# Attention of four heads at a time in 64x64 array tiles, two heads per partition half

## Chip, cores and metric

One core of one Trainium2 chip. The metric is the device time of the program in microseconds (us); lower is better. Every comparison is with runs of the kernel before on the same chip.

In the lines of the profile PE is TensorE, PEld its weight loads, DVE VectorE, ACT ScalarE, POOL GpSimd, whose queue issues the loads, and SP the queue of the output stores and the DMA transposes. The first two numbers are start and duration in us; a bracket such as [3.51 <-DMA x_sb<-xT] is the engine's idle time just before and what ended it. To evict is to copy a result out of PSUM, the memory that TensorE writes; to land is to arrive, for a transfer; a slot is the time that the array needs for one matmul. A burst is the group of loads that one step sends.

## The reference

Attention without softmax, then a mixer block, for 8 batches, 12 heads, 448 tokens and a head size of 64:

```python
scores = scale * np.matmul(q, k.transpose(0, 1, 3, 2))
attn = np.maximum(scores, 0.0) ** 2 / S
x = np.matmul(attn, v)                     # heads side by side: (8, 448, 768)
h = np.maximum(x.transpose(0, 2, 1) @ w_tok1, 0.0) @ w_tok2   # token mix, 448 -> 256 -> 448
u = x + h.transpose(0, 2, 1)
out = u + np.maximum(u @ w_ch1, 0.0) @ w_ch2                  # channel mix, 768 -> 1536 -> 768
```

## The kernel before

It works on a pair of heads per step, 48 steps. `x` comes out of the attention with channels on partitions (`xT`); token 1 needs it with tokens on partitions, so `x_back` turns it, for later steps by a DMA transpose on the SP queue. Channel work (the largest part, 218 us of TensorE) is queued per batch and dealt out in portions by `fill` to keep TensorE busy. Program order is kept on every engine. The parts that matter, cut:

```python
    raw   = ...tile_pool(name="raw", bufs=6)
    ps_att = ...(bufs=2, PSUM)   # scores, two banks each
    ps_acc = ...(bufs=1, PSUM)   # values, one bank
    ps_mm  = ...(bufs=3, PSUM)   # everything else, one bank each

    def scores(s, blocks):       # 128 keys at a time, 64x128 tiles: one head per row half
        for c in blocks:
            for e in range(2):
                h = slice(64 * e, 64 * (e + 1))
                nc.tensor.matmul(ps[:, e, :S], lhsT=sb[h, KO + c*128 : KO + (c+1)*128],
                                 rhs=sb[h, :S], start=True, stop=True)
    # scores_rest: the last 64 keys of both heads in one 128x128 matmul, through the padded kz
    # values: 128x64 tiles; values_rest: one 128x128 matmul through the padded vz

    def x_back(s):
        if s >= XDMA:            # XDMA = 12
            nc.sync.dma_start_transpose(out=x_tiles[s // PG][:, p % PG], in_=xT[b % 2][:, p, :])
            return
        # ... earlier ones by TensorE

    for s in range(NS + 4):      # (cut)
        scores(s, (0, 1)); load_pair(s + PRE); transposes(s + 1); values(s - 1)
        scores(s, (2,)); values_rest(s - 1)
        if s - 1 >= XDMA: x_back(s - 1)
        square(); fill(0.25); scores_rest(s); fill(0.25); square()
        if (s - 3) % PG == PG - 1:
            token2(...)          # of the pairs s-4 and s-3
            if (s - 3) % NP == NP - 1: channel_work(...)     # queues it, and issues six u transposes
        fill(0.25)
        if (s - 2) % PG == PG - 1: token1((s - 2) // PG)     # pairs s-3 and s-2: x sent a step or two ago
        fill(0.25)
```

Of the kernel before, what the change touches and what calls it, by code (L numbers as in the profile page):

```python
# [16 lines left out]
def kernel(  # L17
# [11 lines left out]
    nc = tc.nc  # L29
# [7 lines left out]
    QC = 4  # L37
    QP = S // QC
    KB = 3
    KM = KB * 128  # L40
    KR = S - KM
# [11 lines left out]
    raw = ctx.enter_context(tc.tile_pool(name="raw", bufs=6))  # L53
# [5 lines left out]
    ps_mm = ctx.enter_context(tc.tile_pool(name="ps_mm", bufs=3, space=bass.MemoryType.PSUM))  # L59
# [4 lines left out]
    kz = [consts.tile([128, NP, 128], BF16, name=f"kz{i}") for i in range(2)]  # L64
    vz = [consts.tile([128, NP, 128], BF16, name=f"vz{i}") for i in range(2)]
# [7 lines left out]

    raws = {}

    def load_pair(s):
        b, p = divmod(s, NP)
        h0 = 2 * p
        q_raw = raw.tile([QP, 2, QC, D], BF16, name="q_raw")
        k_raw = raw.tile([128, 2, KB, D], BF16, name="k_raw")  # L80
        v_raw = raw.tile([128, 2, KB, D], BF16, name="v_raw")
        nc.gpsimd.dma_start(  # L82
            out=q_raw.rearrange("p h c d -> p h (c d)"),
            in_=q[b, h0 : h0 + 2].rearrange("h (p c) d -> p h (c d)", c=QC),
        )
        nc.gpsimd.dma_start(  # L86
            out=k_raw.rearrange("p h c d -> p h (c d)"),
            in_=k[b, h0 : h0 + 2, :KM].rearrange("h (p c) d -> p h (c d)", c=KB),
        )
        if s == 0:  # L90
            make_identity(nc, ident)
        if p == 0:
            load_rest(b, kz[b % 2], k)
        nc.gpsimd.dma_start(  # L94
            out=v_raw.rearrange("p h c d -> p h (c d)"),
            in_=v[b, h0 : h0 + 2, :KM].rearrange("h (p c) d -> p h (c d)", c=KB),
        )
        if p == 0:
            load_rest(b, vz[b % 2], v)
        raws[s] = (q_raw, k_raw, v_raw)  # L100

    def load_rest(b, dst, src):
        for e in range(2):
            nc.gpsimd.dma_start(
                out=dst[64 * e : 64 * e + KR, :, D * e : D * (e + 1)],
                in_=src[b].rearrange("(p e) s d -> e s p d", e=2)[e, KM:],
            )

    def load_wt1():
        w = moe_w_tok1.rearrange("(p c) j -> c p j", c=QC)  # L110
        for c in range(QC):
            lo = c * QP
            while lo < (c + 1) * QP:
                hi = min((c + 1) * QP, (lo // 128 + 1) * 128)
                r = lo % 128
                nc.gpsimd.dma_start(
                    out=wt1[r : r + hi - lo, lo // 128, :],
                    in_=w[c, lo - c * QP : hi - c * QP, :],
                )
                lo = hi  # L120
# [13 lines left out]
    def load_wc1(i):  # L134
        n = DC // 2
        nc.gpsimd.dma_start(
            out=wc1[:, :, i * n : (i + 1) * n],
            in_=moe_w_ch1.rearrange("(g p) n -> p g n", p=128)[:, :, i * n : (i + 1) * n],
        )

    def load_wc2(i):
        n = EC // 4
        nc.gpsimd.dma_start(
            out=wc2[:, i * n : (i + 1) * n, :],
            in_=moe_w_ch2.rearrange("(e p) n -> p e n", p=128)[:, i * n : (i + 1) * n, :],
        )


    qkT, at2, squares = {}, {}, []
    KO = S  # L150

    def transposes(s):
        b, p = divmod(s, NP)
        q_raw, k_raw, _ = raws[s]
        ps = ps_mm.tile([128, 1024], BF16, tag="bank", name="qkT_ps")
        blocks = [(c * QP, QP, q_raw[:, :, c, :]) for c in range(QC)]
        blocks += [(KO + c * 128, 128, k_raw[:, :, c, :]) for c in range(KB)]
        blocks.append(
            (KO + KM, 128, kz[b % 2][:, p, :].rearrange("n (h d) -> n h d", h=2))
        )  # L160
        for at, n, src in blocks:
            for h in range(2):
                nc.tensor.matmul(  # L163
                    ps[64 * h : 64 * (h + 1), at : at + n],
                    lhsT=src[:, h, :],
                    rhs=ident[:n, :n],
                    is_transpose=True,
                    start=True,
                    stop=True,
                    skip_group_check=True,  # L170
                )
        sb = attn.tile([128, KO + KM + 128], BF16, name="qkT")
        nc.vector.tensor_copy(sb, ps[:, : KO + KM + 128])  # L173
        qkT[s] = sb

    def relu2(s, key, ps, n):
        at = attn.tile([128, n, S], BF16, tag=f"at{n}", name="at", bufs=3)
        sq = attn.tile([128, n, S], BF16, tag=f"sq{n}", name="sq", bufs=3 * (3 if n == 2 else 1))
        nc.scalar.activation(at, ps[:, :, :S], AF.Relu)  # L179
        squares.append((at, sq))  # L180
        at2[s, key] = sq

    def square():
        for at, sq in squares:
            nc.vector.tensor_tensor(out=sq, in0=at, in1=at, op=ALU.mult)  # L185
        squares.clear()

    def scores(s, blocks):
        sb = qkT[s]
        made = []  # L190
        for c in blocks:
            ps = ps_att.tile([128, 2, 512], FP32, tag="att", name="sc_ps")
            for e in range(2):
                h = slice(64 * e, 64 * (e + 1))
                nc.tensor.matmul(  # L195
                    ps[:, e, :S],
                    lhsT=sb[h, KO + c * 128 : KO + (c + 1) * 128],
                    rhs=sb[h, :S],
                    start=True,
                    stop=True,  # L200
                )
            made.append((c, ps))
        for c, ps in made:
            relu2(s, c, ps, 2)

    def scores_rest(s):
        sb = qkT.pop(s)
        ps = ps_att.tile([128, 1, 512], FP32, tag="att", name="sr_ps")
        nc.tensor.matmul(  # L209
            ps[:, 0, :S],  # L210
            lhsT=sb[:, KO + KM : KO + KM + 128],
            rhs=sb[:, :S],
            start=True,
            stop=True,
        )
        relu2(s, KB, ps, 1)

    accs = {}

    def values(s):  # L220
        v_raw = raws[s][2]
        ps = ps_acc.tile([128, 512], FP32, name="acc_ps")
        for c in range(KB):
            sq = at2.pop((s, c))
            for e in range(2):
                nc.tensor.matmul(  # L226
                    ps[64 * e : 64 * (e + 1), :S],
                    lhsT=v_raw[:, e, c, :],
                    rhs=sq[:, e, :],
                    start=(c == 0),  # L230
                    stop=False,
                    skip_group_check=True,
                )
        accs[s] = ps

    def values_rest(s):
        b, p = divmod(s, NP)
        raws.pop(s)
        ps = accs.pop(s)
        nc.tensor.matmul(  # L240
            ps[:, :S],
            lhsT=vz[b % 2][:, p, :],
            rhs=at2.pop((s, KB))[:, 0, :],
            start=False,
            stop=True,
            skip_group_check=True,
        )
        nc.vector.tensor_scalar(  # L248
            out=xT[b % 2][:, p, :S],
            in0=ps[:, :S],  # L250
            scalar1=float(alpha2),
            scalar2=None,
            op0=ALU.mult,
        )
# [3 lines left out]
    PG = 2  # L258
    XDMA = 12

    def x_back(s):
        b, p = divmod(s, NP)
        if p % PG == 0:
            x_tiles[s // PG] = mix.tile([128, PG, 4, 128], BF16, name="x_sb")
        if s >= XDMA:
            nc.sync.dma_start_transpose(
                out=x_tiles[s // PG][:, p % PG], in_=xT[b % 2][:, p, :]
            )
            return
        ps = ps_mm.tile([128, 1024], BF16, tag="bank", name="x_ps")  # L270
        for c in range(4):
            nc.tensor.matmul(
                ps[:, c * 128 : (c + 1) * 128],
                lhsT=xT[b % 2][:, p, c * 128 : (c + 1) * 128],
                rhs=ident,
                is_transpose=True,
                start=(c == 0),
                stop=(c == 3),
            )
        nc.vector.tensor_copy(  # L280
            x_tiles[s // PG][:, p % PG],
            ps[:, :512].rearrange("n (c d) -> n c d", c=4),
        )

    def token1(i):
        x_sb = x_tiles.pop(i)
        ps = ps_mm.tile([128, JC, PG * 128], FP32, tag="bank", name="t1_ps")
# [9 lines left out]
        r1 = mix.tile([128, JC, PG * 128], BF16, name="r1_sb")  # L297
# [3 lines left out]
    def token2(s):  # L301
        b, p = divmod(s, NP)
# [204 lines left out]
```

## Time and profile before

| | kernel before |
|---|---|
| time, median | 413.6 us (413.0 to 415.0) |
| span of the profiled run | 411.6 us |
| TensorE busy | 388.3 us, 94% |
| first channel matmul at | 58.2 us |
| TensorE clock over the span | 0.98 |

The lines and their reading are in the prediction. Transposes by DMA, whose landing is in the view of the tile `x_sb`:

```profile
L266 SPq DMA_TRANSPOSE x_sb<-xT x36: 1189/1191/2271, 92.2 to 362.6; - x36
DMA to landing us min/median/max: 2.4/4.1/5.6
```

The first line gives the issue on the SP queue in ns (minimum, median, maximum), the second the time from issue to landing.

### The profile page before, as it was taken

How to read it: one execution, taken by the hardware profiler on the slowest of the kernel's cores; microseconds unless marked ns; L12 is line 12 of the kernel's file. 1: busy time of each engine (PE TensorE's matmuls, PEld its weight loads, DVE VectorE, ACT ScalarE, POOL GpSimd, SP SyncE). 2: the span in 40 equal slices, each digit the busy share in tenths (PEclk: the TensorE clock that was granted, in tenths of full speed). 3: DMA queues.
4: the chain of work that ended last, by engine and by line, in shares of the span. 5: the costliest groups of instructions: out<-in, count | busy, mean ns of one | idle time of the engine just before them, and what ended most of it. 6: DMA issues, size and time to landing. Idle time of an engine off the chain costs nothing.

```text
span 411.6 us, 7596 instructions
## 1 busy us (share of the span) xinstructions
PE 388.3 (94%) x3033; PEld 205.4 (50%) x3033; DVE 216.2 (53%) x414; ACT 209.5 (51%) x313; POOL 130.8 (32%) x196
## 2 busy tenths in 40 slices
PE   5856799999999999999999999999999999999995
PEld 2323345555445555555445555555545555555562
DVE  2667774466465566365455665356444755432021
ACT  2745676743674446753575347654566237611400
POOL 8995456244243333243223424235222000000000
PEclk9778999999999999999999999999999999999999
DMA  7999999459946999469955989569953434113323
GB/s 75 119 145 203 187 180 196 57 80 126 167 50 69 137 137 143 45 93 134 134 70 56 146 131 147 57 75 134 149 70 47 93 92 92 24 47 99 60 62 93
DMA packets 101572, 43.44 MB, mean 106 GB/s; under 512 B 83424, under 2 KB 97952, under 8 KB 101536
## 3 DMA queue, kind: packets, MB, share of 16 engines
q0 software_dynamic: 54432, 21.70, 50.2%
q1 hardware_dynamic: 47104, 21.25, 25.3%
q8 instruction: 24, 0.39, 0.4%
q14 instruction: 12, 0.10, 0.1%
HBM read 43.38 MB, written 11.01 MB: 132 GB/s over the span
## 4 chain that ended last, share of the span: by engine, by line
PE 85%; DVE 7%; POOL 4%; issue 1%; DMA 1%; ACT 0%; DVEq 0%; ACTq 0%; POOLq 0%
PE m_ps L345 26%; PE m_ps L363 26%; PE sc_ps L195 8%; PE acc_ps L226 6%; PE qkT_ps L163 6%; PE t_ps L290 5%; PE h_ps L308 3%; PE acc_ps L240 3%; DVE sq L185 3%; PE sr_ps L209 2%; DVE uT_sb L316 1%; DMA wt_nat<-in_moe_w_tok_dram 1%; DVE xT L248 1%; POOL k_raw L86 1%; POOL v_raw L94 1%
## 5 line engine op out<-in xcount | busy, mean ns | idle before, releaser
L179 ACT ACTIVATE at<-sc_ps 128x896 bf16<-128x896 f32 x144 | 122.5, 922 | 60.3 <-PE sc_ps L195 59.9
L345 PE MATMUL m_ps<-uT_sb,wc 128*128 128x448 bf16 x576 | 120.3, 352 | 0.6 <-DVE uT_sb L316 0.5
L363 PE MATMUL m_ps<-wc,r_sb 128*128 128x384 bf16 x672 | 116.7, 326 | 0.0
L185 DVE TENSOR_TENSOR sq<-at 128x896 bf16<-128x896 bf16 x192 | 97.7, 559 | 0.1
L94 POOL DMA_DIRECT2D v_raw<-in_v_dram x48 | 34.5, 719 | 170.1 <-PE sc_ps L195 159.3
L363 PEld LDWEIGHTS <-r_sb 128*128 128x128 bf16 x672 | 65.6, 98 | 44.3 <-issue 0.6
L352 ACT ACTIVATE r_sb<-m_ps 128x448 bf16<-128x448 f32 x96 | 52.1, 543 | 65.9 <-PE m_ps L345 65.9
L345 PEld LDWEIGHTS <-wc 128*128 128x128 bf16 x576 | 56.2, 98 | 49.7 <-issue 1.4
L173 DVE COPY qkT<-qkT_ps 128x960 bf16<-128x960 bf16 x48 | 31.5, 656 | 85.6 <-PE qkT_ps L163 85.6
L371 DVE TENSOR_TENSOR out_sb<-m_ps,u_sb 128x384 f32<-128x384 f32 x56 | 31.1, 555 | 71.4 <-PE m_ps L363 69.2
L195 PE MATMUL sc_ps<-qkT 64*128 64x448 bf16 x288 | 45.6, 365 | 2.5 <-ACT at L179 1.3
L248 DVE TENSOR_SCALAR xT<-acc_ps 128x448 bf16<-128x448 f32 x48 | 29.9, 624 | 29.7 <-PE acc_ps L240 29.7
L226 PE MATMUL acc_ps<-sq,v_raw 128*64 128x448 bf16 x288 | 36.7, 363 | 0.0
L82 POOL DMA_DIRECT2D q_raw<-in_q_dram x48 | 33.0, 688 | 10.8 <-DMA wc<-in_moe_w_ch_dram 9.8
L86 POOL DMA_DIRECT2D k_raw<-in_k_dram x48 | 35.2, 732 | 1.7 <-DMA wc<-in_moe_w_ch_dram 1.7
L179 ACT ACTIVATE at<-sr_ps 128x448 bf16<-128x448 f32 x48 | 26.2, 545 | 16.8 <-PE sr_ps L209 16.8
L290 PE MATMUL t_ps<-x_sb,wt 128*128 128x256 bf16 x192 | 25.7, 278 | 9.0 <-DVE x_sb L280 9.0
L298 ACT ACTIVATE r_sb<-t_ps 128x512 bf16<-128x512 f32 x24 | 14.3, 597 | 38.4 <-PE t_ps L290 38.4
L195 PEld LDWEIGHTS <-qkT 64*128 64x128 bf16 x288 | 10.8, 94 | 37.2 <-issue 35.8
L316 DVE TENSOR_TENSOR uT_sb<-h_ps,xT 128x448 bf16<-128x448 f32 x48 | 27.6, 615 | 2.0 <-PE h_ps L308 2.0
L290 PEld LDWEIGHTS <-wt 128*128 128x128 bf16 x192 | 19.0, 99 | 15.0 <-issue 5.1
L163 PEld LDWEIGHTS <-q_raw 112*64 112x64 bf16 x384 | 12.3, 113 | 22.4 <-issue 18.0
(36 smaller groups left out, 209.0 us busy)
## 6 DMA issues: line engine op xcount, KB each, us to landing
q_raw<-in_q_dram POOLq DMA_DIRECT2D x48, 112.0 KB, 3.9
k_raw<-in_k_dram POOLq DMA_DIRECT2D x48, 96.0 KB, 4.2
v_raw<-in_v_dram POOLq DMA_DIRECT2D x48, 96.0 KB, 2.9
out_dram<-out_sb SPq DMA_DIRECT2D x8, 336.0 KB, 2.8
wc<-in_moe_w_ch_dram POOLq DMA_DIRECT2D x2, 1152.0 KB, 12.0
wc<-in_moe_w_ch_dram POOLq DMA_DIRECT2D x4, 576.0 KB, 9.0
out_dram<-out_sb SPq DMA_DIRECT2D x8, 288.0 KB, 2.7
out_dram<-out_sb SPq DMA_DIRECT2D x8, 240.0 KB, 2.8
```

The lines of the kernel that those rows point to most:

```text
L86: nc.gpsimd.dma_start(out=k_raw.rearrange("p h c d -> p h (c d)"), in_=k[b, h0 : h0 + 2, :KM].rearrange("h (p c) d -> p h (c d)", c=KB),)
L94: nc.gpsimd.dma_start(out=v_raw.rearrange("p h c d -> p h (c d)"), in_=v[b, h0 : h0 + 2, :KM].rearrange("h (p c) d -> p h (c d)", c=KB),)
L163: nc.tensor.matmul(ps[64 * h : 64 * (h + 1), at : at + n], lhsT=src[:, h, :], rhs=ident[:n, :n], is_transpose=True, start=True, stop=True, ...
L179: nc.scalar.activation(at, ps[:, :, :S], AF.Relu)
L185: nc.vector.tensor_tensor(out=sq, in0=at, in1=at, op=ALU.mult)
L195: nc.tensor.matmul(ps[:, e, :S], lhsT=sb[h, KO + c * 128 : KO + (c + 1) * 128], rhs=sb[h, :S], start=True, stop=True,)
L226: nc.tensor.matmul(ps[64 * e : 64 * (e + 1), :S], lhsT=v_raw[:, e, c, :], rhs=sq[:, e, :], start=(c == 0), stop=False, skip_group_check=True,)
L248: nc.vector.tensor_scalar(out=xT[b % 2][:, p, :S], in0=ps[:, :S], scalar1=float(alpha2), scalar2=None, op0=ALU.mult,)
L290: nc.tensor.matmul(ps[:, j, :], lhsT=wt1[:, c, j * 128 : (j + 1) * 128], rhs=x_sb[:, :, c, :], start=(c == 0), stop=(c == 3),)
L345: nc.tensor.matmul(ps[:, :S], lhsT=wc1[:, g, e * 128 : (e + 1) * 128], rhs=uT[:, g, off : off + S], start=(g == 0), stop=(g == CC - 1),)
L352: nc.scalar.activation(r2[:, e, off : off + S], ps[:, :S], AF.Relu)
L363: nc.tensor.matmul(ps[:, :HN], lhsT=r2[:, e, tok], rhs=wc2[:, e, cols], start=(e == 0), stop=(e == EC - 1), skip_group_check=True,)
```

## The change

The intent: fewer TensorE slots and fewer, larger descriptors. Four heads per step, two in each half of the partitions; keys in seven chunks of 64, so four 64x64 tiles of the array work at once and the padded rest (`kz`, `vz`) goes away; every load is one descriptor of 896 bytes (as stored) per partition and head. PSUM is dealt out anew. Cut to the core:

```diff
-    raw = ...bufs=6            +    raw = ...bufs=3
-    ps_mm = ...bufs=3          +    ps_mm = ...bufs=2
+    # ps_acc, bufs=1, now two banks: transposes, values and token 2 share it
+    def load_four(i):          # six loads: q, k, v, two halves each
+        nc.gpsimd.dma_start(out=t[64*r : 64*(r+1)].rearrange("p g c d -> p g (c d)"),
+                            in_=src[b, h0 : h0+2].rearrange("g (p c) d -> p g (c d)", c=QC))
+    def scores(i, c):
+        for r in range(2):
+            for g in range(2):
+                h = slice(64 * g, 64 * (g + 1))
+                nc.tensor.matmul(ps[64*r : 64*(r+1), g, :S], lhsT=sb[h, r, 1, c*64 : (c+1)*64],
+                                 rhs=sb[h, r, 0, :], start=True, stop=True, ...)
+    def x_back(i):             # XDMA = 3, in groups of four heads
+        if i >= XDMA:
+            for r in range(2):
+                nc.sync.dma_start_transpose(out=x_sb[:, r], in_=xT[b % 2][:, 2*d + r, :])
+    for i in range(ND + 2):    # ND = 24
+        scores(i, 0); scores(i, 1); load_four(i + PRE)
+        values(i - 1, range(4)); scores(i, 2); values(i - 1, range(4, QC))
+        values_out(i - 1); x_back(i - 1)
+        square(); fill(1/3)
+        scores(i, 3); scores(i, 4); transposes(i + 1)
+        square(); fill(1/3)
+        token1(i - 1)          # the same step as its x_back
+        scores(i, 5); scores(i, 6)
+        square(); fill(1/6)
+        token2(i - 1)
+        if (i - 1) % DB == DB - 1: channel_work(...)
+        fill(1/6)
```

## The prediction

> **What bounds the kernel now.** I read the page's busy shares and forty slices first, then busy time by stretch, then TensorE's part of the timeline in one steady step, then the waits.
>
> ```profile
> PE 388.3 (94%) x3033; PEld 205.4 (50%) x3033; DVE 216.2 (53%) x414; ACT 209.5 (51%) x313; POOL 130.8 (32%) x196
> ...
> PE   5856799999999999999999999999999999999995
> PEld 2323345555445555555445555555545555555562
> DVE  2667774466465566365455665356444755432021
> ```
>
> TensorE is the only engine near full, but not in the first six slices of 10.3 us. The stretches say the same in numbers (core 0, columns PE, PEld, DVE, ACT, POOL busy us):
>
> ```profile
> 0.00:58.30 58.30, 41.08 (x382) 19.96 (x383) 37.34 (x78) 32.18 (x43) 43.40 (x69) 0.88 1.18 151
> ...
> 200.00:248.00 48.00, 48.00 (x383) 25.56 (x381) 27.33 (x52) 26.17 (x40) 15.64 (x24) 1.00 0.86 103
> ```
>
> So there are two stages. Up to 58.3 us, where the first channel matmul starts (the chain has "58.34 1.14 PE m_ps L345 x6"), the chain alternates between VectorE and TensorE: no channel work fills the gaps yet. From 58.3 to 411 us TensorE never rests; there only its own work, and any new wait in its in-order queue, count. One steady step (one pair of heads, TensorE alone):
>
> ```profile
> 205.09 0.35 PE L345 MATMUL m_ps<-uT_sb,wc 128*128 128x448 bf16 x1
> 205.38 0.55 PE L195 MATMUL sc_ps<-qkT 64*128 64x448 bf16 x4
> 205.86 0.39 PE L163 MATMUL qkT_ps<-ident,q_raw 112*64 112x112 bf16 x8
> 206.08 0.34 PE L163 MATMUL qkT_ps<-ident,k_raw 128*64 128x128 bf16 x6
> 206.25 0.22 PE L163 MATMUL qkT_ps<-ident,kz 128*64 128x128 bf16 x2
> 206.31 0.73 PE L226 MATMUL acc_ps<-sq,v_raw 128*64 128x448 bf16 x6
> 206.97 0.36 PE L195 MATMUL sc_ps<-qkT 64*128 64x448 bf16 x2
> 207.27 0.36 PE L240 MATMUL acc_ps<-sq,vz 128*128 128x448 bf16 x1
> 207.47 1.30 PE L345 MATMUL m_ps<-uT_sb,wc 128*128 128x448 bf16 x6
> 208.60 0.35 PE L209 MATMUL sr_ps<-qkT 128*128 128x448 bf16 x1
> 208.79 1.30 PE L345 MATMUL m_ps<-uT_sb,wc 128*128 128x448 bf16 x6
> ```
>
> Read starts, not durations, since matmuls overlap. Six 448-column matmuls take 207.47 to 208.60: 0.189 us each. From L195's first to L345 is 2.09 us of attention, with L209 2.28 us for a pair, 4.56 us for four heads.
>
> **What the Trainium skill says.** "TensorEngine Tiling (Array Packing)", Key Properties: changing the tiling mode drains the array. The trace agrees: 205.09 to 205.38 is 0.29 us where the same matmul is otherwise followed after 0.189, so a switch costs 0.10 us; 205.86 less two score slots gives the same. A pair has four switches (into 64*128, into 128*64, back, into 128*128). "TensorE: Matmul & The Clock Gate", Part 3, says that tiles of one mode run side by side, about 4 ns apart. The trace agrees for two: four scores take two slots and a switch, 0.48 us, and sixteen transposes 0.45 us. No run yet shows four 64*64 tiles. "DMA: Bandwidth & Descriptors", Specifications, gives 512 B as the least for line rate; the page has 83424 of 101572 packets below that. The larger descriptors are thus right in kind, but after 58 us TensorE's listed waits on loads are nil, so I give them nothing there.
>
> **The change, part by part.** First the matmuls, per four heads. Before: 4.56 us. After, 7 chunks of scores and 7 of values, four matmuls each; if four tiles go in one slot, 14 x 0.189 = 2.65. Transposes: 28 of 128 columns, two by two, at the 0.055 us a pair that the trace has: 0.76. Switches: into the first block, which now holds scores, values, scores, values in one mode, and out; two around the transposes and one before them; two around the last scores: 7 x 0.10 = 0.70. Sum 4.11, a saving of 0.45 us. The rest keeps its size: 96 channel-1 units of 1.137 and 56 channel-2 units of 1.953 us (218.6 together); token 1 0.87 and token 2 0.76 us per four heads.
>
> ACT goes from 144 x 0.922 + 48 x 0.545 = 158.9 us to 168 x 0.922 = 154.9; VectorE's squares from 80.9 + 18.5 to 168 x 0.616 = 103.5. Neither becomes the bound.
>
> Startup: from the program order, VectorE per step of four heads is 7 squares x 0.616 + 2 qkT copies (I take 0.62) + 2 xT x 0.624 + 2 uT x 0.615 + 2 x copies x 0.415 = 8.9 us, and it idles about 1.75 us while values run; 10.6 us per step, against 10.3 for two pairs now (token 1 at 40.40 and 50.70). First scores I put at 10.5 us (k lands later, being two loads, against 7.7 now), the first xT eviction at 21 (after wt2 has landed and been reordered; that landing holds VectorE till 23.7 now), so three steps later channel work starts near 53 instead of 58 us, with 20 fours less a fraction left. Work from there: 218.6 + 21 x (0.87 + 0.76) + 81 (19.5 x 4.11 and the last values) = 334 us.
>
> New waits, from the order of the changed program on each engine:
> - The PSUM pool of accumulators has one buffer, now shared by the transposes, the values and token 2. In seven steps nothing stands between token 2 and the next step's two scores and values. VectorE then still has a square, an output add and two uT adds (0.6 + 0.55 + 2 x 0.615), done some 1.9 us after token 2; TensorE has 0.5 us to do. 7 x 1.4 = 10 us.
> - The third score chunk needs the first one's PSUM buffer. The transposes that stood between are gone. ACT frees it about 1.45 us after the step's start (0.36 matmul, the previous relu, 0.92), TensorE is there at 1.15: 0.3 us in 13 steps, 4 us.
> - Token 1 now comes in the same step as its transposes back by DMA, not a step later. Each takes 1.19 us on the SP queue and 4.1 to land. Ordinarily it lands 8.5 us into the step, and token 1 is due at 9.5 to 10.5. But at a batch's end six u transposes go first:
>
> ```profile
> 195.92 0.79 SPq L382 DMA_DIRECT2D out_dram<-out_sb  x2
> 196.75 8.96 SPq L333 DMA_TRANSPOSE u_sb<-uT_sb  x6
> 205.81 3.70 SPq L266 DMA_TRANSPOSE x_sb<-xT  x2
> ```
>
>   At three of the batch ends they cannot start early, because an output store precedes them; x then lands some 14.4 us after token 2, where token 1 is due at 13: 4 us in all. At the other ends four of the six go early and nothing is lost.
> - The first channel-1 unit waits for uT at those three ends, 1.2 us each, 4 us, and smaller ones 1 us.
> Sum of waits 23 us.
>
> Total: 53 + 334 + 23 + 1 for the end = 411 us of span. The time is 1.9 us above the span now (413.48 against 411.6); I round to **412 us**. So 9 us saved in matmuls, 5 in startup, and most given back in waits.
>
> **Rivals.**
> (a) The waits are smaller than worked out and the saving shows: waits of 10 us give 399 us. For it: each is a difference of two chains of some microseconds, and landings of x range from 2.4 to 5.6 us. Against: one accumulator buffer instead of a three-deep pool is certain.
> (b) Waits grow: u transposes collide with x at every batch end (3 us more at three ends), and two channel buffers instead of three make TensorE wait for VectorE when it does out adds behind squares. That gives 420 to 428 us. For it: VectorE has 8.9 us of attention work per step in clumps. Against: its 53% share, and channel-2 units last 1.95 us against 0.555 of eviction.
> (c) Four tiles don't share one slot. At 0.22 us a group, 20 steps x 14 x 0.03 = 8 us more, 420 us; at two slots the change would cost 20 x 2.65 = 53 us, 465. Against: two tiles by rows and two by columns each run at full rate now, and weight loads keep up at 0.027 us apiece in the transposes.
> (d) The gain lies in the loads: no, since after startup nothing waits for them; in startup at most 3 us.
>
> **Range and chances.** Startup is uncertain by 4 us, waits by 8, tiles by a few upward; together about 8 to 10 either way: 402 to 422. Faster than 405.2 needs the waits halved, 0.22; slower than 421.8 needs (b) or (c), 0.15; the rest 0.63.
>
> **What would show it.** Right: score and value matmuls at four per 0.19 us; the first channel matmul at 50 to 56 us; TensorE idle, hidden now, of about 1 us before values in seven steps, ended by the uT add; token 1 waiting at some batch ends; ACT ending short waits before the third scores. Wrong: groups of four longer than 0.2 us; no idle between 55 us and the end (then about 395 us); or TensorE waits for channel evictions, which I put at none.

## The result

The changed kernel takes 454.3 us (median; its runs spread from 446.4 to 457.4) against 413.6 us: slower by 8.6%, 95% interval 7.3 to 9.9%. A ratio here is the mean time of one kernel's fast runs over that of the other's of the same rounds, so not quite the ratio of the medians. Four of the changed kernel's six runs count as slow, being over 1.5% above its fastest, so its ratio rests on two runs (446.4 and 452.3, mean 449.3). Their mean granted clocks (0.956 and 0.952) do not tell them apart from the slow ones (0.933 to 0.960). The prediction of 412 us (402 to 422) was wrong. The profiled run took 446.4 us, a span of 444.6.

From the page of the changed kernel:

```profile
PE 388.0 (87%) x3585; PEld 206.3 (46%) x3585; DVE 208.9 (47%) x380; ACT 206.7 (46%) x289; POOL 94.3 (21%) x162
...
PE   5877829998699996999979987999979999989995
...
PEclk9599877999989998999999999999989999999999
```

The row for TensorE has dents all along (the sixth slice falls to 2), and the clock row has dents as well. The waits (engine, line, releaser: us in total, times, longest) name them:

```profile
PE t_ps L237 <- DMA x_sb<-xT: 27.9, 12, 8.7
...
PE acc_ps L181 <- DVE uT_sb L265: 9.7, 10, 1.3
...
PE sc_ps L153 <- ACT at L162: 4.4, 17, 0.8
```

L237 is token 1: it waits for the DMA transposes of x. One batch end, TensorE, then the SP queue, then the loads on the POOL queue:

```profile
162.49 0.76 PE L181 MATMUL acc_ps<-at,v_raw 64*64 64x448 bf16 x12
163.19 2.44 PE L295 MATMUL m_ps<-uT_sb,wc 128*128 128x448 bf16 x12
165.56 0.57 PE L153 MATMUL sc_ps<-qkT 64*64 64x448 bf16 x8
166.06 0.58 PE L131 MATMUL qkT_ps<-ident,q_raw 128*64 128x128 bf16 x14
...
166.97 3.58 PE L295 MATMUL m_ps<-uT_sb,wc 128*128 128x448 bf16 x18
174.05 1.86 PE L237 MATMUL t_ps<-x_sb,wt 128*128 128x256 bf16 x8 [3.51 <-DMA x_sb<-xT]
```

```profile
156.25 7.78 SPq L283 DMA_TRANSPOSE u_sb<-uT_sb  x6
164.12 1.18 SPq L328 DMA_DIRECT2D out_dram<-out_sb  x2
165.40 3.33 SPq L213 DMA_TRANSPOSE x_sb<-xT  x2
```

```profile
163.56 1.20 POOL L80 DMA_DIRECT2D v_raw<-in_v_dram  x2 [13.38 <-PE acc_ps L181]
164.73 1.22 POOL L80 DMA_DIRECT2D q_raw<-in_q_dram  x2
165.90 1.24 POOL L80 DMA_DIRECT2D k_raw<-in_k_dram  x2
```

The array side is as intended: eight scores of 448 columns, in four tiles, take 165.56 to 166.06, that is a slot of 0.21 us, one of 0.19 and a mode switch of 0.10. (Groups of four follow each other after 0.189 us in the values and after 0.213 in the scores, throughout this trace.) The loss stands between 170.4 and 174.05. The six loads were released by the values that ended at 163 us, so they started just as x was sent, and x was itself held back, by some 1.5 us here, by six u transposes and an output store on the SP queue. Token 1 then ran at half speed (1.86 us instead of 1.03): the granted clock was 0.5 from 173.7 to 177.1 us. All five half-clock windows between 51 us and the last matmul begin during one of the five longest waits of token 1 or within 1.4 us after it; the sixth longest has none:

```profile
226.18 1.03 PE L237 MATMUL t_ps<-x_sb,wt 128*128 128x256 bf16 x8 [2.42 <-DMA x_sb<-xT]
...
276.66 1.87 PE L237 MATMUL t_ps<-x_sb,wt 128*128 128x256 bf16 x8 [2.61 <-DMA x_sb<-xT]
```

The view of `x_sb`, for this kernel:

```profile
L213 SPq DMA_TRANSPOSE x_sb<-xT x42: 1189/1220/2581, 51.7 to 401.8; - x42
...
DMA to landing us min/median/max: 2.4/4.6/14.2
```

Adding up, in the start times of neighbouring matmuls after 50.9 us, every gap that exceeds the time of the matmul's columns (0.19 us for 448) by more than 0.35 us: 37.3 us in the changed kernel, of which 30.5 directly before token 1; 1.7 us in the kernel before after 55 us. The gaps column of the table below is counted so. The half-clock windows after 51 us add about 8 us (an estimate: 10.2 us and four of 3.4 us in the trace, each counted for half of the time in which TensorE ran).

### The profile page after: what moved, and what is told of

Its sections match the earlier page's. It is cut to its first block, busy times and chain, and to the rows that moved or that the text cites. A ratio compares the mean times of both kernels' runs of the same rounds, so it can differ in the third digit from the quotient of the medians.

```text
span 444.6 us, 8636 instructions
## 1 busy us (share of the span) xinstructions
PE 388.0 (87%) x3585; PEld 206.3 (46%) x3585; DVE 208.9 (47%) x380; ACT 206.7 (46%) x289; POOL 94.3 (21%) x162
## 4 chain that ended last, share of the span: by engine, by line
PE 56%; DMA 17%; DVE 14%; ACT 7%; issue 4%; POOL 0%; SPq 0%; ACTq 0%; DVEq 0%; POOLq 0%
PE m_ps L295 18%; DMA x_sb<-xT 17%; PE m_ps L312 15%; ACT at L162 7%; PE acc_ps L181 6%; PE sc_ps L153 6%; PE t_ps L237 5%; DVE at L168 5%; DVE uT_sb L265 3%; PE qkT_ps L131 3%; DVE xT L195 2%; DVE qkT L141 2%; PE h_ps L257 2%; DVE out_sb L319 1%; DMA k_raw<-in_k_dram 1%
## 5 line engine op out<-in xcount | busy, mean ns | idle before, releaser
L162 ACT ACTIVATE at<-sc_ps 128x896 bf16<-128x896 f32 x168 | 144.1, 918 | 63.9 <-PE sc_ps L153 63.9
L168 DVE TENSOR_TENSOR at<-at 128x896 bf16<-128x896 bf16 x168 | 97.8, 619 | 88.6 <-ACT at L162 88.6
L80 POOL DMA_DIRECT2D v_raw<-in_v_dram x48 | 28.8, 611 | 231.2 <-PE acc_ps L181 228.8
L153 PE MATMUL sc_ps<-qkT 64*64 64x448 bf16 x672 | 54.9, 383 | 5.9 <-ACT at L162 4.4
L237 PE MATMUL t_ps<-x_sb,wt 128*128 128x256 bf16 x192 | 27.4, 290 | 28.7 <-DMA x_sb<-xT 27.9
L181 PE MATMUL acc_ps<-at,v_raw 64*64 64x448 bf16 x672 | 43.4, 369 | 9.7 <-DVE uT_sb L265 9.7
L141 DVE COPY qkT<-qkT_ps 128x896 bf16<-128x896 bf16 x48 | 27.7, 619 | 33.1 <-PE qkT_ps L131 33.1
L237 PEld LDWEIGHTS <-wt 128*128 128x128 bf16 x192 | 18.5, 102 | 37.7 <-issue 18.7
L181 PEld LDWEIGHTS <-v_raw 64*64 64x64 bf16 x672 | 23.2, 111 | 21.5 <-issue 12.6
L153 PEld LDWEIGHTS <-qkT 64*64 64x64 bf16 x672 | 15.9, 108 | 36.0 <-issue 31.5
L80 POOL DMA_DIRECT2D k_raw<-in_k_dram x48 | 29.4, 637 | 1.9 <-issue 1.6
L257 PE MATMUL h_ps<-wt,r_sb 128*128 128x448 bf16 x96 | 22.7, 360 | 1.2 <-DVE qkT L141 1.2
## 6 DMA issues: line engine op xcount, KB each, us to landing
wc<-in_moe_w_ch_dram POOLq DMA_DIRECT2D x4, 1152.0 KB, 17.9
```

The costliest lines, as they stand in the source:

```text
L80: nc.gpsimd.dma_start(out=t[64 * r : 64 * (r + 1)].rearrange("p g c d -> p g (c d)"), in_=src[b, h0 : h0 + 2].rearrange("g (p c) d -> p g ...
L141: nc.vector.tensor_copy(sb[:, :, w, :].rearrange("n r (c p) -> n r c p", c=QC), ps[:, w, : 2 * S].rearrange("n (c r p) -> n r c p", c=QC, ...
L153: nc.tensor.matmul(ps[64 * r : 64 * (r + 1), g, :S], lhsT=sb[h, r, 1, c * 64 : (c + 1) * 64], rhs=sb[h, r, 0, :], start=True, stop=True, s ...
L162: nc.scalar.activation(at, ps[:, :, :S], AF.Relu)
L168: nc.vector.tensor_tensor(out=at, in0=at, in1=at, op=ALU.mult)
L181: nc.tensor.matmul(ps[64 * g : 64 * (g + 1), r, :S], lhsT=v_raw[h, g, c, :], rhs=at[h, g, :], start=(c == 0), stop=(c == QC - 1), skip_gro ...
```

## The experiments

The theory: token 1 stands too close behind the transposes that it needs; x is late because it shares the SP queue with u and the DMA engines with a burst of loads. Rivals: the smaller tiles; the shared PSUM buffers; the mere number of bytes.

| run | median us | ratio to before (95%) | gaps before token 1, us | x landing, median/max us |
|---|---|---|---|---|
| changed kernel | 454.3 | 1.086 (1.073 to 1.099) | 30.5 | 4.6/14.2 |
| token 1 and 2 a step later | 410.8 | 0.994 (0.990 to 0.998) | 0 | 4.9/13.6 |
| x by TensorE, same place | 442.7 | 1.072 (1.067 to 1.078) | 0 | none |
| no loads after the third group | 413.7 | 1.000 (0.996 to 1.004) | 6.4 | 2.4/4.6 |
| u transposes after x | 426.3 | 1.034 (1.028 to 1.039) | 12.7 | 5.0/11.1 |
| five v buffers | 453.2 | 1.093 (1.089 to 1.098) | 35.4 | 2.5/14.0 |
| u after x and five v buffers | 415.2 | 1.004 (1.002 to 1.007) | 6.3 | 2.5/11.2 |
| x by TensorE, after a fill | 429.2 | 1.038 (1.034 to 1.041) | 0 | none |
| kernel before, token 1 a step earlier | 425.1 | 1.028 (1.025 to 1.031) | 13.3 | 4.4/5.3 |
| token 1 later, and reordered | 401.9 | 0.971 (0.968 to 0.974) | 0 | 5.5/15.3 |

All results are correct but that of the run without loads. Its output is wrong, which doesn't matter for the time. The gaps and landings are those of the profiled run. The kernel before, token 1 a step earlier, has one more gap of 0.4 us before token 1, not counted, since the kernel before has it too.

### Token 1 and 2 a step later

```diff
+    def due(i):
+        if 0 <= i - 1 < XDMA: return [i - 1]
+        return [i - 2] if XDMA <= i - 2 < ND else []
-        token1(i - 1)
+        for j in due(i): token1(j)
-        token2(i - 1) ...
+        for j in due(i): token2(j) ...
```

> The changed kernel with token 1 and token 2 of every group whose x comes by DMA moved one step later, nothing else. Main theory (token 1 stands in the same step as its transposes by DMA and waits for their landing: in the changed kernel's trace 30.5 us of TensorE idle before token 1, and about 9 us more in half-clock windows that follow): the idle before token 1 falls under 3 us, the clock stays full after 60 us, the first channel matmul comes some 10 us later, which gives about 5 us back, and the time is 412 to 420. Rival (shared accumulator buffer, smaller tiles or two channel buffers cost the time): over 438.

410.8 us, just below the range: the distance alone is worth some 38 us between fast runs (449.3 and 410.9 on average), and tiles, PSUM pools and loads are untouched. x lands no sooner (median 4.9, longest 13.6 us); nothing waits for it any more, and the clock stays full until the last matmuls. The rivals fall as the main cause; what is left of them is small (0.9 us before the values at seven places, for the shared accumulator). One detail of my expectation was wrong: the first three groups have x from TensorE and were not delayed, so the first channel matmul came at 54.3 us against 50.9, which the trace puts down to a late k load.

### x by TensorE, in two places

```diff
-    XDMA = 3
+    XDMA = ND
```

> All transposes back to tokens on TensorE, none by DMA; token 1 stays where it is. Main theory: no wait for a landing is left, 21 steps get 8 transposes of 0.055 us plus little (9 us of TensorE) and two VectorE copies of 0.42; time 412 to 424. Rival as for the late token: over 440, since TensorE and VectorE only get more work.

442.7 us: a miss. No DMA is waited for, but another wait took its place, at L220, the transposes themselves:

```profile
PEld L220 <- DVE xT L195: 35.4, 48, 1.5
PE x_ps L220 <- DVE xT L195: 17.6, 24, 0.7
```

They stand straight behind the values whose eviction they read. The gap from the last values to them was 1.08 us in 21 steps, and one more of about 0.35 us inside. So this run alone could not tell the theories apart. The second place:

```diff
-            x_back(i - 1)
         square()
         fill(1 / 3)
+        if 0 <= i - 1 < ND:
+            x_back(i - 1)
```

> As the run with all x transposes on TensorE, but they stand after the first fill of the step, not straight after the values whose eviction they need. There the waits were 0.9 and 0.35 us per step beside 0.9 us of transposes. Main theory: those waits go (27 us), 9 to 12 us of transposes stay, time 412 to 420. If it stays over 430 the matmul transposes themselves cost it.

429.2 us, again above what I expected. The transposes themselves (8 of 0.055 us) come to 9 us in 21 steps, and a gap of 0.57 us stays inside each group, 12 us. Its releasers:

```profile
PE x_ps L220 <- ACT r_sb L302: 5.7, 14, 0.4
...
PE x_ps L220 <- DVE out_sb L319: 3.0, 7, 0.4
```

They are evictions of channel work: x needs two of the buffers of `ps_mm`, and the pool now has two. So the smaller pool seems to cost here; no run gave it a third buffer.

### No loads after the third group

```diff
+        if i >= 3:
+            raws[i] = kept[i % 3]
+            return
```

> Wrong result on purpose: q, k and v are loaded for the first three groups only and used again. If the landings are long because the six loads of a step start just when x is sent (median 4.6 us and up to 14.2 in the changed kernel), x lands in 2.5 to 4 us, the idle before token 1 falls to under 12 us and the time to 420 to 430. If the queue order (six u transposes ahead of x) is what counts, the waits at the batch ends stay near 3 us each and the time stays over 435.

413.7 us, below the range that I gave for contention. x lands in 2.4 us:

```profile
DMA to landing us min/median/max: 2.4/2.4/4.6
```

What is left is the wait from the queue order: 1.66, 1.80 and 1.55 us at three batch ends and 0.4 to 0.55 at three others. That is near what I had worked out for the changed kernel, three waits of about 1.4 us, and so is the time, but both by luck. Counted from token 2's first matmul, the second x was sent after 12.1 to 12.4 us where the prediction has 10.3 (14.4 less 4.1), and it landed 1.7 us sooner after that. In the total, too much for waits and too little for work cancel (see below). What the run does show is that the loads made small waits large: 6.4 us of gaps before token 1 without them, 30.5 with them.

How they do it can be counted in the trace's DMA records of the changed kernel, packets that start in a stretch around the batch end shown above:

```
us               load packets (896 B)   transpose packets (256 B)
168.0 to 172.5   439                    642      143 per us
172.5 to 173.5   24                     382
```

After 173.5 none of either is left to start. The transposes are not stopped; they run between the loads, and more than twice as fast once those have ended. (x was sent at 165.4; up to 168 the SP queue's packets were those of the output store ahead of it, and 30 of its 128 came later still. Behind a store but without loads, at the same batch end of the run without loads, the pair landed in 3.5 and 4.4 us; here it took 7.2 and 8.1.)

### u transposes after x

```diff
     def channel_work(b):
-        u_back(b)
+        backs.append(b)
...
             x_back(i - 1)
+        while backs: u_back(backs.pop())
```

> The six u transposes of a batch end go to the queue in the next step, after that step's x. If the queue order makes the waits, the waits of 2.6 to 4.2 us at the batch ends (19 us in all with their half clock excluded, without the first of 8.9) vanish and the time falls by 15 to 30 us; the first of 8.9 us shrinks only a little, since two u transposes stood before it. If contention with loads makes them, most stay and the time falls by under 8 us.

426.3 us, some 24 us less between fast runs. The waits at batch ends shrank from 8.9, 4.2, 3.7, 2.6, 2.8 and 3.0 us to 6.2 at the first, none or under 2.1 at the others; those in ordinary steps (0.7 to 1.6 us before, 0.6 to 1.0 now) mostly stayed. So the queue order counts too.

### Five v buffers

```diff
-            t = raw.tile([128, 2, QC, D], BF16, name=f"{name}_raw")
+            t = raw.tile([128, 2, QC, D], BF16, name=f"{name}_raw", bufs=5 if name == "v" else 3)
```

> The changed kernel with five v buffers instead of three, all data and results kept. The burst of six loads of a step is then released by the transposes in the middle of the step, not by the end of the values, so it starts some 3 us after x is sent, not with it. If the burst beside x makes the long landings, the median landing of x falls to under 3.5 us and the time to 416 to 428. If it is the mere number of bytes per step, the landing stays over 4.3 us and the time over 440.

453.2 us: right on the landing (median 2.5 us), wrong on the time. Ordinary steps no longer wait at all. At batch ends it is worse, 5.2 to 7.0 us at four of them, because the burst, now released by the transposes in mid step, falls just where the late x is sent:

```profile
218.94 2.52 SPq L283 DMA_TRANSPOSE u_sb<-uT_sb  x2
...
220.32 1.19 POOL L80 DMA_DIRECT2D q_raw<-in_q_dram  x2 [11.58 <-PE qkT_ps L131]
...
221.48 1.22 POOL L80 DMA_DIRECT2D k_raw<-in_k_dram  x2
...
221.56 2.57 SPq L213 DMA_TRANSPOSE x_sb<-xT  x2
...
222.64 1.24 POOL L80 DMA_DIRECT2D v_raw<-in_v_dram  x2
```

### Both

> The changed kernel with both: five v buffers (the burst of loads starts in mid step) and the u transposes of a batch end after the next step's x. Token 1 keeps its early place. Each alone left x behind something: behind the six u transposes and then the burst (453 us), or beside the burst (426 us). Theory that x waits for what stands ahead of it, the SP queue's transposes and the burst's packets on the shared DMA engines: x now goes ahead of both, the idle before token 1 stays under 4 us after 70 us, median landing under 3 us, time 407 to 418. If it stays over 424, landings have another cause.

415.2 us, as expected, with token 1 in its early place and all bytes loaded, so the mere number of bytes is not the cause. The two cures do not simply add: the gaps before token 1 fall by 18 us with the first alone, rise by 5 with the second alone, and fall by 24 with both. A single wait is left, the first:

```profile
PE t_ps L237 <- DMA x_sb<-xT: 6.1, 1, 6.1
```

It comes from the first x, sent at 52 us. In the changed kernel a weight load of 1152 KB had been issued at 45 us (loads of that size have a median landing of 17.9 us) and the next burst at 52 us; that they delay this x is likely by the same account, but no run took them away alone.

### The kernel before, with token 1 a step earlier

```diff
-        if 0 <= s - 2 < NS and (s - 2) % PG == PG - 1:
-            token1((s - 2) // PG)
+        if 0 <= s - 2 < XDMA and (s - 2) % PG == PG - 1:
+            token1((s - 2) // PG)
+        if XDMA <= s - 1 < NS and (s - 1) % PG == PG - 1:
+            token1((s - 1) // PG)
```

> The kernel before with token 1 alone moved forward a step for x that comes by DMA, so that it stands some 5 us after the x of its second pair is sent. Main theory (the distance from x to token 1 is what the change lost): idle before token 1 of 1 to 2 us at each of 18 places and of 8 us at batch ends, time 430 to 465. Rival (the tiles and the buffers of the changed kernel cost the time): within 1% of before.

425.1 us: the same wait appears in the old kernel, with its old tiles, buffers and loads, so the distance alone makes it. It is smaller than I expected (430 to 465), 0.6 to 1.5 us at ten places and 2.7 at one; no landing exceeded 5.3 us. That its bursts are three loads and not six is the likely reason, which this run does not test.

```profile
PE t_ps L290 <- DMA x_sb<-xT: 10.8, 10, 2.6
```

### Token 1 later, and the step reordered

```diff
-            values(i - 1, range(4))
+            values(i - 1, range(QC))
             scores(i, 2)
-            values(i - 1, range(4, QC))
...
+        for j in due(i): token1(j)
         fill(1 / 3)
-        token1(i - 1)
+        for j in due(i): token2(j) ...      # with channel_work
         scores(i, 5); scores(i, 6)
         square()
-        fill(1 / 6); token2(i - 1) ...; fill(1 / 6)
+        fill(1 / 3)
```

> Token 1 and 2 a step later as before, and in addition token 1 before the second fill, token 2 after it (so that channel work stands between it and the next values, which share its PSUM buffer), and the third scores after all values. If the remaining waits are those predicted from the shared buffer (0.9 us seen at 7 places) and from the score buffer (0.2 to 0.34 us at 19), they vanish, 8 to 10 us: time 399 to 404, faster than both kernels. If they only move elsewhere, 408 to 412.

401.9 us (399.9 to 403.1), 2.9% faster than the kernel before. The page:

```profile
PE   5675879997999999999999999999999999999994
```

After 102 us no gap over 0.4 us is left: the waits on the shared accumulator are gone, since a fill stands between token 2 and the next values. Of the 11.2 us by which the span is shorter than that of the kernel before, 9.6 lie before the first channel matmul (48.6 us against 58.2). The rest of the span is only 1.6 us shorter. It holds more attention work and 6.3 us of gaps, all before 102 us. The saving in attention matmuls is there: from start to start, gaps taken out, those after the first channel matmul take 79.6 us for 20 groups of scores, 19 of transposes and 21 of values, against 87.8 for 19.5, 18.5 and 19.5 in the kernel before. Most of it is the tiles': with token 1 moved and the order otherwise kept, they take 81.2 us for 19.6, 19 and 20.

## Why the prediction was wrong

- **What bounds the kernel: right.** From the start of channel work TensorE's own queue decides; the loss is in gaps of that queue and in the half clock around them.
- **Matmuls: right.** Four tiles share a slot, two groups and a switch in 0.50 us; switches cost 0.10 us; token and channel units kept their sizes. A little of rival (c) came true: groups of scores take 0.213 us, over the 0.2 named as a sign of being wrong, at most 3.4 us in all (an estimate: 20 steps of 7 groups, 0.024 us each).
- **Count of work: 8 us short.** Span less start, gaps, smaller waits and half clock (444.6 - 50.9 - 37.3 - 5 - 8) is about 343 us, not 334 and 1 for the end. Some 5 of these lie behind the start of the last matmul (438.7 of 444.6 us), where the prediction has 1; the kernel before has 5.3 there too. Counted in the same way the kernel before comes to 345 us for a stretch that takes 353, so this is a fault of the counting and not of the change. The prediction's own differences from the kernel before, 9 and 5 us saved and 23 of waits, give 422 and not 412. Trying the count on the kernel before would have shown it. (Its last step is off too: 411 and 1.9 make 413.)
- **Startup: nearly right.** First channel matmul at 50.9 us, predicted near 53; VectorE's steps took 9.8 us, predicted 10.6.
- **Accumulator buffer: right in kind, high in size.** 0.9 us at six places and 1.4 at the end, 6.8 us after startup; predicted 10.
- **Score buffer: right.** A mean excess of 0.20 us in 19 steps, 3.7 us; predicted 4.
- **Token 1: this is the step that failed.** "x then lands some 14.4 us after token 2, where token 1 is due at 13: 4 us in all. At the other ends ... nothing is lost." Measured: 30.5 us, plus some 8 us of half clock that I had not counted at all. The 30.5 fall into four parts.
  - The first x: 8.9 us, with landings of 12.5 and 14.2. Here the cause is in part open (see the run with both cures).
  - The three batch ends that the prediction names: 9.8 us instead of 4. Here the landing was about as assumed, 3.3 to 4.4 us for the second x; it was sent too late, 11.6 to 12.8 us after token 2's first matmul instead of 10.3, against a token 1 due at 13.2. The six u transposes ahead of it held the queue for 7.9 to 8.9 us (8.96 already in the prediction's own lines), where six times its 1.19 is 7.1.
  - The other batch ends, where nothing was to be lost: 3.7, 2.8 and 0.35 us. In the first two the second x landed in 7.2 us.
  - Five ordinary steps: 0.7 to 1.6 us each, 5.1 in all, with landings of about 6 us.

  I took the median landing of the kernel before, 4.1 us, as if it belonged to the transposes. The run without loads shows a median of 2.4 us; beside six loads and behind a store the pair in the view of one batch end took 7.2 and 8.1 us:

```profile
DMA to landing us min/median/max: 7.2/7.6/8.1
```

- **Loads: the sentence that hid it.** "After 58 us TensorE's listed waits on loads are nil, so I give them nothing there." The waits list shows what TensorE waits for, not what slows the thing it waits for. The changed program order on POOL said that six loads, no longer three, are freed by the end of the values, the moment at which x is sent.
- **Rival (b)** named the collision at every batch end but put it at "3 us more at three ends"; its 428 us was still far off: it had nothing for the first x, the ordinary steps, the half clock or the work missing from the count. Rival (d) fell as expected, and (c) but for the small part above.
- **Where a reader could have stopped me:** in the old order the x of a pair was sent a step or two ahead of token 1, steps of 7.7 us, so some 6 us were in hand after a landing of 4.1; in the new order 1 to 2 us. A margin of one or two microseconds on a landing that ranged from 2.4 to 5.6 us should have widened the range upward, and the range had no case for it.

## What to carry to other kernels

When a change shortens the distance from a DMA to its consumer in an in-order queue, compare that distance with the worst landing beside everything else that the new order sends at that moment, not with the old median. Ask of each burst of loads what releases it: here two v buffers more moved it from the end of the values to the transposes in mid step. The two cures, more distance (one step) or a clear queue ahead of x, came to 411 and 415 us. With the distance no wait for x was left; with the clear queue one of 6.1 us was.

## What the Trainium skill lacked or had wrong

- "DMA: Bandwidth & Descriptors", section Issuing engines are not separate DMA queues, says that DMAs of all issuers run on the same 16 engines and interleave. The runs agree (transpose packets run between load packets). The page gives no size for what this does to a transpose: 2.4 us median landing without loads, 4.6 with them, 7.2 to 8.1 for a pair beside six loads of 112 KB and behind an output store (3.5 to 4.4 behind a store without the loads).
- "TensorEngine Tiling (Array Packing)", Key Properties, says that a change of mode drains the array but not what that costs: 0.10 us at each switch here. Nor has the page a measurement of four 64x64 tiles: here four matmuls of 448 columns take one slot, 0.189 us in the values and 0.213 in the scores, where two 64x128 tiles took 0.200 in the kernel before.
- "TensorE: Matmul & The Clock Gate", section Why this matters for your kernels, advises no idle of more than about 3 us between bursts. Here half clock began during an idle of 2.6 us (before 276.7 us in the changed kernel), and in the last run (58.8 us) during the second of two idles of 0.9 and 1.6 us close together. One of 2.4 us (226.2 us in the changed kernel) and one of 2.6 us (104.8 us in the kernel before with token 1 a step earlier) brought none. So less than the 3 us can be too much, and these runs show no sharp limit.
